# Who spreads the inverse row sums, and where: VectorE into a buffer of its own, with two steps of the opening moved forward

## The chip, the cores and the metric

The kernel runs on one core of a Trainium2 chip. The metric is the device time of one execution in microseconds (us). A core has five engines that run their own instruction streams and wait for each other by semaphores: TensorE (PE, matrix products; PEld is its loading of weights), VectorE (DVE), ScalarE (ACT), GpSimd (POOL) and SyncE (SP, which issues most transfers).

## The reference, cut to what matters

Three stages follow each other: attention with a local window, a dense layer with the mish activation, and a mixture of eight experts of which each token takes one.

```python
scores = scale * q @ k.T + bias          # 2 batches, 8 heads, 768 tokens, 64 per head
scores = where(keep, scores, -1e9)       # 96 local and 8 global keys
a = exp(scores - max(scores))
a = a / (sum(a) + 1e-9)
x = (a @ v)                              # 1536 tokens x 512
h = x @ w_in                             # 512 -> 2048
g = h * tanh(log1p(exp(h)))
x = g @ w_out                            # 2048 -> 512
e = argmax(x @ w_gate); p = softmax(x @ w_gate)[e]
out = p * (max(x @ w1[e], 0) @ w2[e])    # 8 experts, 512 -> 1024 -> 512
```

The change touches the division of `a` by its sum. The kernel multiplies `a @ v` by the inverse of the sum instead.

## The kernel before, in words

**Attention.** The 1536 tokens are 12 tiles of 128. A step `s` is half a tile: four of its eight heads. A step goes through scores on TensorE (`a_S`, L289), row maxima on VectorE (`a_max`, L302), exponentials and row sums on ScalarE (`a_exp`, L313), eight transposes on TensorE (`a_T`, L338 and L340), their copies to SBUF as `PT` on ScalarE (`a_Tev`, L353), and the products with `v` on TensorE (`a_V`, L375), which leave `av`, transposed: channels on the partitions, tokens along the row.

**The inverse row sums.** After the second step of tile `t`, `a_recip(t)` (L318, L319) turns the eight sums per token into their inverses on VectorE, and GpSimd spreads each of them over the 64 channels of its head (L321), into a tile `rs`. The sums have tokens on the partitions and `av` has channels there, so `a_R(t)` transposes the spread tile on TensorE (L327) and ScalarE copies the result back over `rs` (L328). Then `a_x(t)` multiplies `av` by `rs` in place (L388, VectorE), casts the product to the high part `xh` (L389, ScalarE) and subtracts to get the low part `xl` (L390, VectorE). `rs` has one buffer: the spread of a tile waits until L390 of the tile before is through.

**Scaling q.** `prep_qk(t)` scales the q of a tile (L264), on VectorE for tile 0 and on GpSimd for the others. From the fourth tile on it is placed behind the last spread on GpSimd (`gorder`).

**The mixture layer, first part.** Units `u` of one weight block by 256 tokens (two tiles): 24 products `hp` (L421) from `xh`, `xl` and a weight pair `wpair`, the mish chain on ScalarE and VectorE (L448 to L480), and 12 products `acc` (L440) two units later. The weights are 64-bit numbers that are cut to fp32 and split on VectorE (L167, L169, L171, L207) and ScalarE (L205), a chunk at a time; these are called conversion below. Units 0 to 9 run interleaved with the attention of tiles 2 to 11, two steps per unit. From unit 12 on, `x_reload` brings `xh` and `xl` back from DRAM on GpSimd's queue (L403).

**What sets the order.** In the opening (steps 0 to 4, up to `a_x(1)`) the order on TensorE, ScalarE, VectorE and GpSimd is that of the code. It holds warm-up products (`fill`, L843) that compute nothing. Behind the opening a scheduler orders each engine by priorities and its own estimates. Every engine runs its stream in order, and each wait holds up all that stands behind it.

**The prefill.** 24 transfers from one tile of zeros, `z` (L592 to L598), on SP's queue clear the experts' lists in DRAM. `z` comes from the pool `xe` under the tag `x2`, which has three buffers in turn and later holds rows on their way to the experts.

Of the kernel before, what the change touches and what calls it, by code (L numbers as in the profile page):

```python
# [8 lines left out]
F32 = mybir.dt.float32  # L9
# [9 lines left out]
B, H, S, D = 2, 8, 768, 64  # L19
NT, DM, DFF = B * S, H * D, 2048  # L20
# [15 lines left out]
ROW = DM + 2  # L36
# [5 lines left out]
def moe_kernel(ctx, tc, q, k, v, n_global, n_local, w_in, w_out, w_gate, w1, w2, out, dbg=None):  # L42
    nc = tc.nc
# [8 lines left out]
    xe = main.enter_context(tc.tile_pool(name="xe", bufs=3))  # L52
# [6 lines left out]
    ident = const.tile([128, 128], F32, name="ident")  # L59
# [36 lines left out]
    gorder = [None]  # L96
# [117 lines left out]
    at = actx.enter_context(tc.tile_pool(name="at", bufs=2, side="right"))  # L214
# [65 lines left out]
    rbs = {}  # L280
# [28 lines left out]
    def a_exp(s, q_):  # L309
        t, pr = divmod(s, 2)  # L310
        w = geom(t)[1]
        h = 4 * pr + q_
        nc.scalar.activation(out=Ps[s][:, q_, 0:w], in_=Ps[s][:, q_, 0:w], func=AF.Exp,  # L313
                             bias=mxs[s][:, q_:q_ + 1], scale=-1.0, accum_out=rcs[t][:, h:h + 1])

    def a_recip(t):
        su = rcs.pop(t)
        nc.vector.tensor_scalar_add(su, su, 1e-9)  # L318
        nc.vector.reciprocal(su, su)  # L319
        rbs[t] = at.tile([128, 4, 128], F32, tag="rs", name="rs", bufs=1)  # L320
        gorder[0] = nc.gpsimd.tensor_copy(rbs[t].rearrange("p a (b c) -> p (a b) c", c=64),  # L321
                                          su.unsqueeze(2).to_broadcast([128, H, 64])).ins

    def a_R(t):
        rb = ps.tile([128, 4, 128], F32, tag="b", name="rb")
        for p_ in range(4):
            nc.tensor.transpose(rb[:, p_, :], rbs[t][:, p_, :], ident)  # L327
        nc.scalar.copy(rbs[t], rb)  # L328

    pts = {}  # L330
# [504 lines left out]
    with tc.manual_schedule(engines={mybir.EngineType.PE, mybir.EngineType.Activation, mybir.EngineType.DVE, mybir.EngineType.Pool}), tc.tile_pool(name="tmp0", bufs=1, side="right") as tmp0:  # L835
# [34 lines left out]
        for s in range(NS):  # L870
            for q_ in range(2):
                a_exp(s, q_)
            if s:
                fill(4)
                a_T(s - 1, 0)
                a_T(s - 1, 1)
# [4 lines left out]
            if s == 0:  # L881
                for _ in range(6):
                    next(b1, None)
            if s == 4:
                a_x(0)
            if s + 1 < NS:
                a_max(s + 1, 0)
# [17 lines left out]
            if s:  # L905
                fill(3)
                a_V(s - 1)
            if s in (2, 4):
                a_R(s // 2 - 1)
            if s in (2, 3):  # L910
                next_conv(2)
            if s in (1, 2):
# [15 lines left out]
    s = NS  # L928
# [116 lines left out]
    for u in range(u0, NU + 2):  # L1045
        pl, bl, jl = units[u - 2]
        rt = bl - 1 if pl == 2 and bl > 0 else None
        if u < NU:
            p, b, j = units[u]
# [143 lines left out]
    with tc.If(slow > 0):  # L1193
        dense = nc.values_load(flag[0:1, 1:2], min_val=0, max_val=1)
        with tc.If(dense > 0):
            xd = dr.tile([NT, DM], F32, name="xd")
            sld = dr.tile([1, H], F32, name="sld")
            with tc.tile_pool(name="fa", bufs=1) as fa, tc.tile_pool(name="fap", bufs=1, space=PSUM) as fap:
# [13 lines left out]
                for b in range(B):  # L1212
                    with tc.For_i(0, H, 1) as hi_:
# [10 lines left out]
                        for i in range(TPB):  # L1224
# [27 lines left out]
                            su = fa.tile([128, 1], F32, name="fsu")  # L1252
# [15 lines left out]
            with tc.tile_pool(name="fm", bufs=1) as fm, tc.tile_pool(name="fmp", bufs=1, space=PSUM) as fmp:  # L1268
# [16 lines left out]
                with tc.For_i(0, NTILE, 1) as ti_:  # L1285
# [24 lines left out]
                    x2 = fm.tile([128, ROW], F32, name="fx2")  # L1310
# [94 lines left out]
```

## Time and profile before

| | |
|---|---|
| time, three runs | 615.55, 611.99, 615.64 us (median 615.55) |
| profiled execution | 612.52 us, of it 610.8 us span from the first to the last instruction |
| TensorE busy | 588.1 us (96%) |
| VectorE busy | 477.2 us (78%) |
| ScalarE busy | 379.3 us (62%) |
| GpSimd busy | 96.5 us (16%) |
| granted TensorE clock | 0.995 of full speed on average |

Durations below come from the profiled execution. Times are counted from the first instruction. A busy share says little about a stage by itself: matrix products are pipelined, so TensorE can be called busy while it is slowed, and an engine that is idle may have nothing to do. What counts is which engine is waited for in a stretch, and what stands behind the waiting instruction.

### The profile page before, as it was taken

What the parts mean: (1) busy time and instruction counts of PE and PEld (TensorE: products, weight loads), DVE (VectorE), ACT (ScalarE), POOL (GpSimd) and SP (SyncE); (2) the same over time, 40 slices, a digit from 0 to 9 for tenths busy, and PEclk for the clock granted to TensorE, in tenths of its full rate; (3) what the DMA queues carried; (4) which work ended last, traced back from release to release, by engine and by line L of the source; (5) the groups of instructions that cost most, each with busy time, mean ns of one, the idle gap of its engine ahead of it and who ended that gap; (6) DMA issues with size and microseconds to landing.
All of it is one profiled execution on the core that took longest, in us unless ns stands there. A gap on an engine that the chain in (4) does not pass through costs nothing.

```text
span 610.8 us, 12116 instructions
## 1 busy us (share of the span) xinstructions
PE 588.1 (96%) x4374; PEld 528.5 (87%) x4374; DVE 477.2 (78%) x1143; ACT 379.3 (62%) x882; POOL 96.5 (16%) x167
## 2 busy tenths in 40 slices
PE   7989999999999999999999999988999999999994
PEld 6868777777799899999899898878999999999994
DVE  5999999985589999877667677755896678887942
ACT  3768787878767655655555555455664466676731
POOL 3131111120100100000201111121201212113111
PEclk8999999999999999999999999999999999999998
DMA  7975677699768665431332210287676384586300
GB/s 216 313 225 184 225 237 238 204 269 295 208 217 281 195 204 173 139 137 35 105 97 77 88 53 36 56 294 243 210 253 222 134 304 150 207 302 213 123 18 21
DMA packets 54904, 109.93 MB, mean 180 GB/s; under 512 B 5708, under 2 KB 12876, under 8 KB 54835
## 3 DMA queue, kind: packets, MB, share of 16 engines
q1 hardware_dynamic: 49138, 90.18, 44.7%
q0 software_dynamic: 5696, 18.89, 9.3%
q8 instruction: 36, 0.59, 0.4%
q14 instruction: 34, 0.27, 0.1%
HBM read 84.64 MB, written 25.10 MB: 180 GB/s over the span
## 4 chain that ended last, share of the span: by engine, by line
PE 68%; DVE 12%; ACT 7%; DMA 6%; issue 3%; SPq 1%; POOL 1%; DVEq 0%; POOLq 0%; ACTq 0%
PE hp L421 21%; PE acc L440 18%; PE bhp L704 4%; PE bacc L704 4%; DMA bst<-in_moe_w_dram 3%; DVE bw L157 3%; PE av L375 2%; ACT P L313 2%; PE bhp L705 2%; PE bacc L705 2%; DMA xg<-x,dsi 2%; PE warm L843 1%; PE sp L289 1%; PE bhp L707 1%; PE bacc L707 1%
## 5 line engine op out<-in xcount | busy, mean ns | idle before, releaser
L421 PE MATMUL hp<-xh,wpair 128*128 128x256 f32 x768 | 151.6, 287 | 1.9 <-ACT xh L389 1.9
L421 PEld LDWEIGHTS hp<-xh,wpair 128*128 128x128 f32 x768 | 122.1, 188 | 7.6 <-ACT xh L389 3.3
L440 PE MATMUL acc<-wpair,gh 128*128 128x512 f32 x384 | 123.8, 400 | 1.4 <-ACT gh L477 1.4
L421 PE MATMUL hp<-xl,wpair 128*128 128x256 f32 x384 | 108.7, 283 | 0.9 <-DVE xl L390 0.8
L440 PEld LDWEIGHTS acc<-wpair,gh 128*128 128x128 f32 x384 | 68.1, 188 | 16.3 <-issue 2.5
L157 DVE TENSOR_TENSOR bw<-bst,bw 128x512 fp32r<-128x512 f32 x112 | 72.9, 685 | 11.4 <-ACT bw L156 10.8
L448 ACT ACTIVATE e<-hp 128x512 f32<-128x512 f32 x48 | 28.7, 599 | 80.7 <-PE hp L421 80.7
L156 ACT CAST bw<-bst 128x512 fp32r<-128x512 f32 x112 | 64.6, 621 | 21.0 <-PE bhp L708 9.4
L440 PE MATMUL acc<-wpair,gl 128*128 128x512 f32 x192 | 75.4, 393 | 0.0
L421 PEld LDWEIGHTS hp<-xl,wpair 128*128 128x128 f32 x384 | 72.3, 188 | 3.1 <-DVE xl L390 1.9
L704 PE MATMUL bhp<-xc,bw 128*128 128x352 f32 (+4 forms) x192 | 59.3, 364 | 0.7 <-DVE t L739 0.6
L704 PE MATMUL bacc<-hc,bw 128*128 128x352 f32 (+4 forms) x192 | 59.2, 363 | 0.0
L313 ACT ACTIVATE P<-P,mx 128x232 f32<-128x232 f32 (+1 forms) x96 | 44.8, 469 | 16.6 <-DVE mx L302 16.6
L705 PE MATMUL bhp<-xc,bw 128*128 128x176 f32 (+4 forms) x192 | 48.4, 252 | 0.0
L705 PE MATMUL bacc<-hc,bw 128*128 128x176 f32 (+4 forms) x192 | 48.4, 252 | 0.0
L458 DVE SCALAR_TENSOR_TENSOR n<-n,r 128x512 f32<-128x512 f32 x48 | 33.0, 688 | 16.1 <-ACT r L456 15.9
L440 PEld LDWEIGHTS acc<-wpair,gl 128*128 128x128 f32 x192 | 36.1, 188 | 7.5
L480 DVE SCALAR_TENSOR_TENSOR gl<-n,gh 128x512 fp32r<-128x512 f32 x48 | 33.1, 690 | 11.4 <-ACT gh L477 10.2
L452 ACT ACTIVATE n<-e 128x512 f32<-128x512 f32 x48 | 30.3, 632 | 12.0 <-DVE e L450 11.7
L704 PEld LDWEIGHTS bhp<-xc,bw 128*128 128x128 f32 x192 | 36.1, 188 | 1.7 <-DVE t L739 0.8
L705 PEld LDWEIGHTS bacc<-hc,bw 128*128 128x128 f32 x192 | 36.7, 191 | 0.0
L705 PEld LDWEIGHTS bhp<-xc,bw 128*128 128x128 f32 x192 | 36.7, 191 | 0.0
(192 smaller groups left out, 1270.2 us busy)
## 6 DMA issues: line engine op xcount, KB each, us to landing
bst<-in_moe_w_dram SPq DMA_DIRECT2D x56, 512.0 KB
wst<-in_moe_w_in_dram SPq DMA_DIRECT2D x16, 512.0 KB
wst<-in_moe_w_out_dram SPq DMA_DIRECT2D x16, 512.0 KB
xl<-xs POOLq DMA_DIRECT2D x12, 512.0 KB, 4.2
xh<-xs POOLq DMA_DIRECT2D x12, 512.0 KB, 4.9
xpl<-xps SPq DMA_DIRECT2D x24, 256.0 KB
xg<-z SPq DMA_DIRECT2D x24, 224.9 KB
w0f<-in_moe_w_dram SPq DMA_DIRECT2D x8, 512.0 KB
```

The lines of the kernel that those rows point to most:

```text
L156: nc.scalar.copy(hi, src)
L157: nc.vector.tensor_sub(lo, src, hi.bitcast(F32))
L313: nc.scalar.activation(out=Ps[s][:, q_, 0:w], in_=Ps[s][:, q_, 0:w], func=AF.Exp, bias=mxs[s][:, q_:q_ + 1], scale=-1.0, accum_out=rcs[t][ ...
L375: nc.tensor.matmul(av[64 * j:64 * j + 64, 2 * pr + i, :], lhsT=lh, rhs=rh, start=(c == 0), stop=(c == 1))
L421: yield lambda f=f, kk=kk, wi=wi, xx=xx, cs=cs: nc.tensor.matmul(hp[:, f, :], lhsT=w[:, wi, kk, cs], rhs=xx[:, kk, :], start=(kk == 0 and ...
L440: yield lambda f=f, o=o, cs=cs, gi=gi, wi=wi, first=first, last=last: nc.tensor.matmul(accs[b][o], lhsT=gi[:, cs], rhs=w[:, wi, f, :], sta ...
L448: nc.scalar.activation(out=e, in_=hp, func=AF.Exp, scale=-1.0)
L452: nc.scalar.activation(out=n, in_=e, func=AF.Square)
L458: nc.vector.scalar_tensor_tensor(out=n, in0=n, scalar=0.25, in1=r, op0=ALU.add, op1=ALU.mult)
L480: nc.vector.scalar_tensor_tensor(out=gl, in0=n, scalar=-(2.0 ** -80), in1=gh.bitcast(F32), op0=ALU.mult, op1=ALU.subtract)
L704: nc.tensor.matmul(o[:, 0:2 * cap], lhsT=wh, rhs=xc, start=first, stop=False)
L705: nc.tensor.matmul(o[:, 0:cap], lhsT=wl, rhs=xh, start=False, stop=last)
```

## The change

Three things. First, the spread is a VectorE copy into a tile `sp_` from the pool `xe` (tag `x2`), so the source of the transposes is no longer the buffer that `x` is built in; `rs` is now only the target of ScalarE's copy. With the spread gone from GpSimd, `gorder` stays at the last bias copy, and the scaling of q no longer stands behind spreads. Second, in the opening `a_R(0)` and `a_R(1)` stand at the start of steps 2 and 4 instead of behind the products with `v` there. Third, `a_x(0)` stands in step 3 instead of step 4.

```diff
@@ a_recip, a_R
         nc.vector.reciprocal(su, su)
-        rbs[t] = at.tile([128, 4, 128], F32, tag="rs", name="rs", bufs=1)
-        gorder[0] = nc.gpsimd.tensor_copy(rbs[t].rearrange("p a (b c) -> p (a b) c", c=64),
-                                          su.unsqueeze(2).to_broadcast([128, H, 64])).ins
+        sp_ = xe.tile([128, ROW], F32, tag="x2", name="sp_")[:, 0:DM]
+        nc.vector.tensor_copy(sp_.rearrange("p (a b) -> p a b", b=64), su.unsqueeze(2).to_broadcast([128, H, 64]))
+        rbs[t] = sp_
 
     def a_R(t):
         rb = ps.tile([128, 4, 128], F32, tag="b", name="rb")
+        sp_ = rbs[t]
         for p_ in range(4):
-            nc.tensor.transpose(rb[:, p_, :], rbs[t][:, p_, :], ident)
+            nc.tensor.transpose(rb[:, p_, :], sp_[:, p_ * 128:p_ * 128 + 128], ident)
+        rbs[t] = at.tile([128, 4, 128], F32, tag="rs", name="rs", bufs=1)
         nc.scalar.copy(rbs[t], rb)
@@ the opening, for s in range(NS)
             for q_ in range(2):
                 a_exp(s, q_)
+            if s in (2, 4):
+                a_R(s // 2 - 1)
             if s:
                 fill(4)
                 a_T(s - 1, 0)
...
-            if s == 4:
+            if s == 3:
                 a_x(0)
...
                 a_V(s - 1)
-            if s in (2, 4):
-                a_R(s // 2 - 1)
```

Line numbers of the changed kernel are higher by one or two from L321 on: its copy is L321, its transposes are L328, and what was L388 to L390 is L390 to L392. Three places show what that does to the streams.

**Place 1, x of tile 0.** VectorE behind the maxima of step 3, before and then after. L167, L169, L171 and L207 are conversion, L388 (L390 after) is x, L390 (L392 after) is `xl`, and L302 begins the maxima of step 4.

```order
L207 TENSOR_TENSOR wpair_0_302<-cv,wpair_0_302 128x512
L167 TENSOR_SCALAR cv<-wst 128x512 x2
L169 SCALAR_TENSOR_TENSOR cv<-wst,cv 128x512 x2
L171 SCALAR_TENSOR_TENSOR cv<-wst,cv 128x512 x2
L302 ISA P,mx<-sp,ndist 128x232
```

```order
L207 TENSOR_TENSOR wpair_0_302<-cv,wpair_0_302 128x512
L167 TENSOR_SCALAR cv<-wst 128x512 x2
L169 SCALAR_TENSOR_TENSOR cv<-wst,cv 128x512 x2
L171 SCALAR_TENSOR_TENSOR cv<-wst,cv 128x512
L390 TENSOR_TENSOR rs<-av,rs 128x512
L171 SCALAR_TENSOR_TENSOR cv<-wst,cv 128x512
L392 TENSOR_TENSOR xl<-rs,xh 128x4x128
L302 ISA P,mx<-sp,ndist 128x232
```

The product and the difference of tile 0 now stand ahead of the maxima of step 4. ScalarE at the same place, before and then after; L353 (L355 after) copies `PT` of step 2, L389 (L391 after) is `xh`, L205 conversion.

```order
L313 ACTIVATE P,su<-P,mx 128x232 x2
L328 COPY rs<-rb 128x512
L313 ACTIVATE P,su<-P,mx 128x232 x2
L353 COPY PT<-pt 104x512
L353 COPY PT<-pt 128x512
L205 CAST wpair_0_302<-cv 128x512
```

```order
L205 CAST wpair_0_302<-cv 128x512
L313 ACTIVATE P,su<-P,mx 128x232 x4
L391 CAST xh<-rs 128x4x128
L355 COPY PT<-pt 104x512
L355 COPY PT<-pt 128x512
L205 CAST wpair_0_302<-cv 128x512
```

The cast of tile 0 moved to a place directly ahead of the two copies of `PT`; the copy of `rb`, L328, moved forward out of this piece.

**Place 2, x of tile 1.** VectorE from the sums of tile 1 to its product (L388 before, L390 after), before and then after.

```order
L318 TENSOR_SCALAR su<-su 128x8
L319 RECIPROCAL su<-su 128x8
L207 TENSOR_TENSOR wpair_0_302<-cv,wpair_0_302 128x512
L388 TENSOR_TENSOR rs<-av,rs 128x512
L207 TENSOR_TENSOR wpair_0_506<-cv,wpair_0_506 128x512
L167 TENSOR_SCALAR cv<-wst 128x512
L390 TENSOR_TENSOR xl<-rs,xh 128x4x128
L169 SCALAR_TENSOR_TENSOR cv<-wst,cv 128x512
L167 TENSOR_SCALAR cv<-wst 128x512
L171 SCALAR_TENSOR_TENSOR cv<-wst,cv 128x512
L169 SCALAR_TENSOR_TENSOR cv<-wst,cv 128x512
L388 TENSOR_TENSOR rs<-av,rs 128x512
```

```order
L318 TENSOR_SCALAR su<-su 128x8
L319 RECIPROCAL su<-su 128x8
L321 COPY sp__413<-su 128x512
L207 TENSOR_TENSOR wpair_0_302<-cv,wpair_0_302 128x512
L167 TENSOR_SCALAR cv<-wst 128x512
L207 TENSOR_TENSOR wpair_0_508<-cv,wpair_0_508 128x512
L169 SCALAR_TENSOR_TENSOR cv<-wst,cv 128x512
L167 TENSOR_SCALAR cv<-wst 128x512
L171 SCALAR_TENSOR_TENSOR cv<-wst,cv 128x512
L169 SCALAR_TENSOR_TENSOR cv<-wst,cv 128x512
L171 SCALAR_TENSOR_TENSOR cv<-wst,cv 128x512
L390 TENSOR_TENSOR rs<-av,rs 128x512
```

The copy came in, the product and the difference of tile 0 are gone from here, and one more L171 stands ahead of the product of tile 1.

**Place 3, the transposes of tile 1.** TensorE from the products with `v` of step 2 to the scores of step 5 (L289), before and then after. L843 (L845 after) are warm-ups, L338 and L340 (L340 and L342 after) the transposes of P of step 3, L327 (L328 after) those of the spread sums.

```order
L375 MATMUL av<-PT,vv 64x128 x8
L843 MATMUL warm<-ident 128x128 x4
L338 MATMUL pt<-ident,P 104x128 x4
L340 MATMUL pt<-ident,P 128x128 x4
L843 MATMUL warm<-ident 128x128 x3
L375 MATMUL av<-PT,vv 64x128 x8
L327 MATMUL rb<-ident,rs 128x128 x4
L289 MATMUL sp<-kT,qr 128x232 x4
```

```order
L377 MATMUL av<-PT,vv 64x128 x8
L328 MATMUL rb<-ident,sp__413 128x128 x4
L845 MATMUL warm<-ident 128x128 x4
L340 MATMUL pt<-ident,P 104x128 x4
L342 MATMUL pt<-ident,P 128x128 x4
L845 MATMUL warm<-ident 128x128 x3
L377 MATMUL av<-PT,vv 64x128 x8
L289 MATMUL sp<-kT,qr 128x232 x4
```

The transposes moved ahead of one whole step of P and of its products with `v`; those of tile 0 moved in the same way one tile earlier.

On GpSimd the 12 spreads are gone, the scalings of q now follow each other in pairs of tiles, and the memset of `z`, which stood at the start of the stream, stands behind the last of them.

## Rows read from the trace of the kernel before

**Rows 1.** The page, busy time of each engine, its share of the span, and instructions
```profile
PE 588.1 (96%) x4374; PEld 528.5 (87%) x4374; DVE 477.2 (78%) x1143; ACT 379.3 (62%) x882; POOL 96.5 (16%) x167
```

**Rows 2.** Windows: stretch, its length, busy us of each engine, clock, DMA
```profile
core 0: us, PE busy (x) PEld busy (x) DVE busy (x) ACT busy (x) POOL busy (x), PEclk, DMA share, GB/s
40.00:120.00 80.00, 77.33 (x637) 61.67 (x635) 78.15 (x212) 66.74 (x179) 12.12 (x15) 1.00 0.65 214
120.00:160.00 40.00, 38.95 (x312) 30.78 (x308) 27.95 (x85) 30.30 (x84) 4.99 (x5) 1.00 0.98 285
```

**Rows 3.** Timeline around the first spread: start, duration, engine, line, operation, tiles
```profile
16.83 0.38 DVE L167 TENSOR_SCALAR cv<-wst 128x512 int32<-128x512 int32 x1
17.24 0.98 DVE L169 SCALAR_TENSOR_TENSOR cv<-wst,cv 128x512 int32<-128x512 int32 x1
17.64 1.48 POOL L264 TENSOR_TENSOR qr<-qr,qsc 128x512 f32<-128x512 f32 x1
18.25 1.41 DVE L171 SCALAR_TENSOR_TENSOR cv<-wst,cv 128x512 int32<-128x512 int32 x1
```

**Rows 4.** Timeline of the opening, TensorE; in brackets idle time before and its releaser
```profile
15.80 1.54 PE L375 MATMUL av<-PT,vv 8*64 8x128 f32 x16
...
26.75 1.10 PE L375 MATMUL av<-PT,vv 104*64 104x128 f32 x16
...
30.41 1.10 PE L375 MATMUL av<-PT,vv 104*64 104x128 f32 x16
31.60 0.66 PE L327 MATMUL rb<-ident,rs 128*128 128x128 f32 x4
...
33.17 1.16 PE L945 MATMUL wm<-ident 128*128 128x128 f32 x8
35.18 0.39 PE L421 MATMUL hp<-xh,wpair 128*128 128x256 f32 x1 [0.85 <-ACT xh L389]
...
35.91 0.39 PE L421 MATMUL hp<-xl,wpair 128*128 128x256 f32 x1
```

**Rows 5.** Timeline of the opening, the other engines
```profile
24.08 1.28 DVE L171 SCALAR_TENSOR_TENSOR cv<-wst,cv 128x512 int32<-128x512 int32 x2
...
24.74 1.06 ACT L353 COPY PT<-pt 104x512 f32<-104x512 f32 x2
...
27.38 0.17 DVE L318 TENSOR_SCALAR su<-su 128x8 f32<-128x8 f32 x1
...
30.63 0.91 POOL L321 COPY rs<-su 128x512 f32<-128x512 f32 x1 [11.52 <-PE warm L843]
...
33.80 0.68 DVE L388 TENSOR_TENSOR rs<-av,rs 128x512 f32<-128x512 f32 x1
```

**Rows 6.** L450: its group (ns shortest/median/longest), then timeline rows beside GpSimd's
```profile
L450 DVE TENSOR_SCALAR e<-e x48: 412/427/1296, 42.2 to 391.9; 128x512 f32<-128x512 f32 x48
...
67.59 1.04 POOL L264 TENSOR_TENSOR qr<-qr,qsc 128x512 f32<-128x512 f32 x1
67.67 1.24 DVE L450 TENSOR_SCALAR e<-e 128x512 f32<-128x512 f32 x1 [0.52 <-ACT e L448]
...
108.84 0.83 DVE L450 TENSOR_SCALAR e<-e 128x512 f32<-128x512 f32 x1
...
135.25 0.96 DVE L450 TENSOR_SCALAR e<-e 128x512 f32<-128x512 f32 x1 [0.79 <-ACT e L448]
```

**Rows 7.** Groups of one line: ns shortest/median/longest, first and last start, form
```profile
L321 POOL COPY rs<-su x12: 613/874/1124, 17.0 to 161.1; 128x512 f32<-128x512 f32 x12
...
L264 DVE TENSOR_TENSOR qr<-qr,qsc x1: 684/684/684, 8.5 to 8.5; 128x512 f32<-128x512 f32 x1
```

**Rows 8.** Prefill and first re-load: timeline rows, and the page's us to landing (last)
```profile
127.94 10.29 SPq L598 DMA_DIRECT2D xg<-z  x14
...
162.21 0.92 POOL L403 DMA_DIRECT2D xl<-xs  x1
...
179.12 0.28 PE L421 MATMUL hp<-xh,wpair 128*128 128x256 f32 x1
...
xh<-xs POOLq DMA_DIRECT2D x12, 512.0 KB, 4.9
```

## The prediction

> **What bounds the kernel now.** I read the page first, then the windows by stage, then the timeline of the opening. On the page TensorE is busy for 96% of the span [rows 1], so a change can only pay where TensorE waits or fills time. The windows say where that may be [rows 2]. From 40 to 120 us VectorE is busy for 78.15 of 80 us and TensorE for 77.33: both are all but full, and VectorE has 1.85 us to spare in the whole stretch. From 120 to 160 us VectorE has 12 us to spare (27.95 of 40 busy) and TensorE 1.05. Soon after, attention ends and TensorE carries the rest, so what TensorE has lost by then stays in the time. The reader should keep two questions: when does the first mixture product start in the opening, and does VectorE get more work before 120 us?
>
> In the opening TensorE goes from one attention step to the next with warm-up products between them [rows 4]. The first product of the mixture layer starts at 35.18 us, after a wait of 0.85 for xh of token tile 1; the first that needs xl of that tile follows at 35.91. What is late there is x of tile 1 (VectorE, 33.80 [rows 5]), behind its transposes (31.60 [rows 4]), behind GpSimd's spread (30.63 [rows 5]). The sums of tile 1 were taken up at 27.38 [rows 5]. GpSimd was idle, but its spread of tile 1 goes into the one buffer that still holds x of tile 0, and waits until that x has been split.
>
> **The change, part by part.**
>
> *Price of one spread.* On GpSimd it took 0.61 to 1.12 us, 12 times [rows 7]. The trace has no VectorE copy of a spread operand. From below, one-source VectorE instructions of 512 elements took 0.38 and 0.41 [rows 3, 6]; from above, the one that multiplies by a spread operand took 0.68 [rows 7]. A copy has one source, so I take 0.41 and keep 0.68 for the range. Twelve copies are 4.9 us of VectorE work, about nine of them before 120 us. The Trainium skill ("VectorE: DVE Perf Modes", the perf-mode tier table) gives an fp32 copy within SBUF two elements a cycle; by it the price would be the lower one, and 0.38 for a one-source shift agrees [rows 3].
>
> *What VectorE gets back.* A VectorE instruction that starts while GpSimd works is longer by what GpSimd has left: L450 takes 0.41 at its shortest, and 1.24 where it starts 0.08 us after L264 [rows 6]. I went through all VectorE instructions of 512 elements from 17 to 170 us. Five were stretched by the spread itself (first L169 at 17.24, 0.98 instead of 0.68; last L450 at 108.84, 0.83 instead of 0.41 [rows 3, 6]): 1.6 us together. These go. Six were stretched by the scaling of q, L264, that GpSimd does right after the spread (first L171 at 18.25, 1.41 instead of 0.68; last L450 at 135.25, 0.96 [rows 3, 6]): 4.7 us together. The scaling stays on GpSimd, no longer behind a spread, and runs as soon as its q has landed, two tiles in a row; it will meet other VectorE instructions, and I count its 4.7 us as unchanged. The Trainium skill ("SBUF — State Buffer", who interferes with whom) has it that whoever comes second waits for the whole instruction, which these rows agree with, and that VectorE instructions with one SBUF input outside the two-port modes are spared. That is the mechanism of the first rival.
>
> *The opening, in the order of the changed rows.* The transposes of tile 0 (about 0.5 us) stand behind the values of step 0, which end at 17.3 [rows 4]. The copy follows the reciprocal at about 16.9 and ends at 17.3 to 17.6, so TensorE waits 0 to 0.3 us. Scores and maxima of step 3 come 0.5 later, and so does VectorE's conversion work behind them.
>
> Now x of tile 0 stands between two L171 (a pair from 24.08 on before [rows 5]). It starts at 24.08 + 0.6 + 0.5 = 25.2 and ends at 25.8. On ScalarE the cast to xh now stands ahead of the two copies of PT that started at 24.74 [rows 5], and waits for x: cast 25.8 to 26.4, PT 26.4 to 27.5. TensorE needs both for the values of step 2, which began at 26.75 [rows 4]: they begin at 27.5. Behind PT on ScalarE stand a conversion cast (0.6) and the last two exponentials of tile 1 (1.0), until 29.1; the sums were taken up at 27.38 before. Sum, reciprocal and copy on VectorE are done at 29.9. TensorE has finished its values at 28.6 and waits 1.3 us for that copy, with the warm-ups, P and the values of step 3 queued behind the transposes. From values to values it needed 26.75 to 30.41, 3.7 us [rows 4]: the values of step 3 come at 27.5 + 3.7 + 1.3 + 0.5 = 33.0. From there to the end of the warm-ups it was 30.41 to 34.3 with 0.6 for the transposes that are gone from this place [rows 4]: 33.0 + 3.3 = 36.3. So the first mixture product starts at about 36.3 instead of 35.18.
>
> Is x of tile 1 there by then? After the copy VectorE has eight conversion instructions first (six at 0.6, two at 0.35: 4.4 us): 29.9 + 4.4 = 34.3, x to 35.0, xh to 35.6, then one conversion, one maximum, xl to 36.6. So xh is in time for 36.3, and xl comes at 36.6; before it was 35.18 and 35.91. The opening loses **0.7 to 1.1 us; I take 1.0**. The wait at 35 us goes, but two of its size take its place earlier: for PT at 27 and for the copy of tile 1 at 29. In exchange VectorE has done one more conversion by then.
>
> *From 40 to 120 us.* Seven copies at 0.41 are 2.9; two of the five relieved instructions lie here, 0.6. VectorE's work grows by 2.3 us, and it has 1.85 to spare [rows 2]. TensorE loses 0.4 if all of that can be used, 2.3 if none: I take 0.5, near the lower end, because TensorE is nearly full itself and because conversions, which are needed only later, stand further back in the changed order. After 120 us nothing: the last three copies lie in 12 us of spare time [rows 2]; without it they would cost 1.2.
>
> *What else moves.* The prefill's zero tile shares a pool of three buffers with the new tile, so its memset now stands behind the last scaling on GpSimd, and the 24 writes from it on SP's queue (14 of them from 127.94 on [rows 8]) come 20 to 30 us later, among the first re-loads of x. The first re-load has 17 us from its issue (162.21) to its use (179.12) and lands in about 5 [rows 8], so I cost it at nothing; without that cover TensorE would stop at 179 us.
>
> **Sum.** 1.0 and 0.5 are 1.5 us more. The profiled execution took 612.5, so it would be 614.0. The three runs lie between 612.0 and 615.6 with a mean of 614.4, and the profiled one stands 3 below their median of 615.55. I set the sum on the mean: **615.9 us**.
>
> **The rivals.**
> - *Faster, the spared meetings.* The scaling now mostly meets the maxima of L302 or idle time, and its 4.7 us go with the spreads' 1.6. VectorE gains 6.3 and pays 4.9, 1.4 net; an L450 such as that of 67.67, between product and mish, gets shorter by 0.83 twice, and an opening that breaks even saves the 1.5 of the sum: 614.4 - 1.4 - 1.7 = 611.3. For it: L302 reads PSUM and is never stretched in the trace. Against: nearly all else on VectorE reads two SBUF tiles, and the scalings come in pairs. Chance 0.18.
> - *Slower, the queues of ScalarE and VectorE.* The copy costs 0.68 and VectorE's growth goes through one for one: 7 x 0.68 - 0.6 = 4.2; the opening loses the whole 1.7 us by which PT is late. That is 5.9: 620.3. It decides from a copy of 0.6 us on. Chance 0.12.
> - *The prefill's writes delay the re-loads.* Sixteen of the writes fall between 169 and 182 us; a re-load would have to take over three times its 5 us. Then perhaps 3 us more than the forecast's mean, 617.4. Chance 0.08.
> - The forecast has the rest, 0.62.
>
> **Chances.** The range reaches from the first rival to the second: 610.4 to 620.6, about 0.9 below and 0.3 above their centres. A measurement of this kernel can tell about 1% (6.2 us) from no change. Faster by that needs 609.4, beyond the first rival: 0.04. Slower needs 621.7, the upper part of the second: 0.10. The rest is 0.86.
>
> **What would show it.** Right: the copy at 0.38 to 0.45 us; TensorE waiting for ScalarE's PT at about 27 and for the copy at about 29 us; the first mixture product at 36 to 37; L264 on GpSimd in pairs. Wrong: a copy of 0.6 or more; a first product before 35; few long instructions on VectorE and less than 80 us for the work from 40 to 120; TensorE waiting at 179 us.

## The result and the profile after

The changed kernel took 617.86 us (median of 22 runs, 613.78 to 622.01), the kernel before 613.22 us on the same chip (22 runs, 611.55 to 616.01). The ratio is 1.0068, with a 95% interval of 1.0048 to 1.0087: 0.7% slower, 4.2 us between the means of the runs. The forecast was 615.9 us and no change beyond 1%.

The profiled execution of the changed kernel took 619.03 us, of it 617.2 us span. The page of it, busy time of each engine:

```profile
PE 589.6 (96%) x4374; PEld 530.9 (86%) x4374; DVE 480.7 (78%) x1155; ACT 380.2 (62%) x882; POOL 85.4 (14%) x155
```

Against [rows 1] twelve instructions have gone from GpSimd to VectorE. TensorE is busy 1.5 us longer in a span that is 6.4 us longer, so it has waited more. The first question is where. The first mish exponential of each unit (L448 before, L450 after) serves as a mark along the kernel:

| unit | before, us | after, us | later by |
|---|---|---|---|
| 0 | 40.83 | 44.96 | 4.13 |
| 3 | 81.58 | 87.19 | 5.61 |
| 6 | 121.65 | 126.38 | 4.73 |
| 9 | 161.95 | 166.18 | 4.23 |
| 24 | 249.96 | 254.19 | 4.23 |
| 47 | 391.29 | 395.51 | 4.22 |

In this execution all of it is there at the first mixture unit. The stretch with the interleaved attention moves the loss up and down and ends 0.1 us worse. From unit 9 to unit 47 nothing changes. (The last 2.2 us of the span came at 400 to 412 us, in the hand-over to the experts, where this execution had a lower clock, 0.72 from 406 to 412 us against 1.00 before. That the table's 4.23 us equal the 4.2 us between the means is partly chance: 1.0 of them belongs to this execution's clock in the first 14 us, as shown below.) The windows of after, with the columns of [rows 2]:

```profile
core 0: us, PE busy (x) PEld busy (x) DVE busy (x) ACT busy (x) POOL busy (x), PEclk, DMA share, GB/s
40.00:120.00 80.00, 75.86 (x634) 61.41 (x636) 76.94 (x221) 64.52 (x174) 8.78 (x10) 1.00 0.64 211
120.00:160.00 40.00, 39.19 (x316) 31.18 (x314) 30.06 (x92) 33.18 (x89) 0.78 (x4) 1.00 0.52 179
```

VectorE is not fuller from 40 to 120 us than before (76.94 against 78.15). The opening on TensorE, to be laid beside [rows 4] (start, duration, engine, line, tiles; in brackets the idle time before and its releaser):

```profile
16.83 1.54 PE L377 MATMUL av<-PT,vv 8*64 8x128 f32 x16
...
19.19 0.66 PE L328 MATMUL rb<-ident,sp__286 128*128 128x128 f32 x4 [0.83 <-DVE sp__286 L321]
...
28.87 1.36 PE L377 MATMUL av<-PT,vv 104*64 104x128 f32 x16
31.73 1.04 PE L328 MATMUL rb<-ident,sp__413 128*128 128x128 f32 x4 [1.49 <-DVE sp__413 L321]
32.56 1.91 PE L845 MATMUL warm<-ident 128*128 128x128 f32 x8
34.27 1.06 PE L340 MATMUL pt<-ident,P 128*104 128x128 f32 x4
...
36.40 1.10 PE L377 MATMUL av<-PT,vv 104*64 104x128 f32 x16
...
39.32 0.37 PE L423 MATMUL hp<-xh,wpair 128*128 128x256 f32 x1
...
39.94 0.38 PE L423 MATMUL hp<-xl,wpair 128*128 128x256 f32 x1
```

TensorE now waits twice for VectorE's copies. Behind the second wait stand the transposes of the exponentials of step 3 (34.27) and their product (36.40). The first mixture product starts at 39.32 instead of 35.18. ScalarE and VectorE in the same stretch, beside [rows 3, 5]:

```profile
17.81 1.04 POOL L264 TENSOR_TENSOR qr<-qr,qsc 128x512 f32<-128x512 f32 x1
...
18.16 0.98 DVE L321 COPY sp__286<-su 128x512 f32<-128x512 f32 x1
...
27.71 0.62 ACT L391 CAST xh<-rs 128x512 fp32r<-128x512 f32 x1 [3.02 <-DVE rs L390]
28.24 1.06 ACT L355 COPY PT<-pt 104x512 f32<-104x512 f32 x2
...
30.80 0.17 DVE L318 TENSOR_SCALAR su<-su 128x8 f32<-128x8 f32 x1 [0.47 <-ACT P L313]
31.24 0.43 DVE L321 COPY sp__413<-su 128x512 f32<-128x512 f32 x1
...
31.96 2.39 POOL L264 TENSOR_TENSOR qr<-qr,qsc 128x512 f32<-128x512 f32 x2 [12.33 <-DMA qr<-in_q_dram]
32.30 1.15 DVE L167 TENSOR_SCALAR cv<-wst 128x512 int32<-128x512 int32 x1
33.37 1.52 DVE L207 TENSOR_TENSOR wpair<-cv,wpair 128x512 fp32r<-128x512 f32 x1
...
37.68 0.68 DVE L390 TENSOR_TENSOR rs<-av,rs 128x512 f32<-128x512 f32 x1
```

The reader should see three things. ScalarE stands idle for 3.02 us ahead of xh of tile 0, with PT behind it. The first copy meets a scaling of q and takes 0.98 instead of 0.43. And a pair of scalings lies between the second copy and x of tile 1 and stretches two conversions there by 0.73 and 0.84.

A last view is the copy's and the mish instruction's group (ns shortest/median/longest):

```profile
L321 DVE COPY sp__601<-su x1: 415/415/415, 44.7 to 44.7; 128x512 f32<-128x512 f32 x1
...
L452 DVE TENSOR_SCALAR e<-e x48: 414/427/634, 45.6 to 396.1; 128x512 f32<-128x512 f32 x48
```

Eleven of the twelve copies took 0.41 to 0.43 us, like the one shown. The mish instruction that GpSimd stretched to 1.30 before [rows 6] now takes 0.63 at most.

### The profile page after: what moved, and what is told of

Same layout as the page of the kernel before. It is cut to its first block, busy times and chain, and to the rows that moved or that the text cites. A ratio compares the mean times of both kernels' runs of the same rounds, so it can differ in the third digit from the quotient of the medians.

```text
span 617.2 us, 12103 instructions
## 1 busy us (share of the span) xinstructions
PE 589.6 (96%) x4374; PEld 530.9 (86%) x4374; DVE 480.7 (78%) x1155; ACT 380.2 (62%) x882; POOL 85.4 (14%) x155
## 4 chain that ended last, share of the span: by engine, by line
PE 75%; DVE 10%; ACT 5%; DMA 4%; issue 3%; SPq 1%; POOL 1%; DVEq 0%; POOLq 0%; ACTq 0%
PE hp L423 22%; PE acc L442 19%; PE bhp L706 5%; PE bacc L706 5%; PE av L377 3%; PE bhp L707 2%; PE bacc L707 2%; PE sp L289 2%; DMA bst<-in_moe_w_dram 2%; PE bhp L709 1%; PE bacc L709 1%; PE bacc L711 1%; PE bhp L711 1%; PE bacc L710 1%; PE bhp L710 1%
## 5 line engine op out<-in xcount | busy, mean ns | idle before, releaser
L450 ACT ACTIVATE e<-hp 128x512 f32<-128x512 f32 x48 | 28.7, 599 | 79.9 <-PE hp L423 79.9
L156 ACT CAST bw<-bst 128x512 fp32r<-128x512 f32 x112 | 64.5, 620 | 19.6 <-PE bhp L710 9.6
L442 PEld LDWEIGHTS acc<-wpair,gl 128*128 128x128 f32 x192 | 36.3, 189 | 7.6
L707 PEld LDWEIGHTS bacc<-hc,bw 128*128 128x128 f32 x192 | 36.7, 191 | 0.0
L707 PEld LDWEIGHTS bhp<-xc,bw 128*128 128x128 f32 x192 | 36.7, 191 | 0.0
L706 PEld LDWEIGHTS bacc<-hc,bw 128*128 128x128 f32 x192 | 36.1, 188 | 0.6
```

The costliest lines, as they stand in the source:

```text
L156: nc.scalar.copy(hi, src)
L442: yield lambda f=f, o=o, cs=cs, gi=gi, wi=wi, first=first, last=last: nc.tensor.matmul(accs[b][o], lhsT=gi[:, cs], rhs=w[:, wi, f, :], sta ...
L450: nc.scalar.activation(out=e, in_=hp, func=AF.Exp, scale=-1.0)
L706: nc.tensor.matmul(o[:, 0:2 * cap], lhsT=wh, rhs=xc, start=first, stop=False)
L707: nc.tensor.matmul(o[:, 0:cap], lhsT=wl, rhs=xh, start=False, stop=last)
```

## The experiments

Two numbers are read from each profile. One is the first mixture product. The other is **TensorE's idle time from 16 us to the first mish exponential of unit 9**, because that is the stretch in which the marks above move and TensorE carries what follows. It comes from one window per kernel. Here are those of before and of after: stretch, its length, busy time of TensorE, and the other engines as above.

```profile
16.00:161.95 145.95, 141.17 (x1171) 112.79 (x1168) 129.56 (x368) 114.57 (x313) 25.05 (x32) 1.00 0.77 242
```

```profile
16.00:166.18 150.18, 142.56 (x1179) 114.96 (x1178) 133.66 (x384) 116.25 (x316) 15.06 (x23) 0.99 0.62 204
```

TensorE is idle for 4.78 us before (145.95 less 141.17) and for 7.62 after: 2.84 us more. The other 1.39 of the 4.23 us is busy time. Of it 1.0 was work left over at 16 us: the sums of tile 0 were taken up at 17.52 instead of 16.51, since the granted clock was 0.50 of full speed from 8 to 14 us (its lower level throughout) where before it was 0.72 on average. The remaining 0.4 is slower work from 32 to 36 us: the clock was at 0.50 from 32 to 34 us, after TensorE had been busy for only 0.51 us of the 2 us before. The windows of the changed kernel, TensorE alone (stretch, length, busy time, clock, DMA):

```profile
8.00:14.00 6.00, 4.72 (x28) 0.50 1.09 304
30.00:32.00 2.00, 0.51 (x8) 0.96 0.85 246
32.00:34.00 2.00, 2.00 (x11) 0.50 0.13 53
```

| run | what it is | ratio (95%) | first product, us | TensorE idle, us |
|---|---|---|---|---|
| before | | 1 | 35.18 | 4.78 |
| after | | 1.0068 (1.0048 to 1.0087) | 39.32 | 7.62 |
| e1_zlate | before, zero tile late | 0.9999 (0.9968 to 1.0029) | 34.70 | 5.62 |
| e2_zfill | after, identity as late as before | 1.0066 (1.0034 to 1.0098) | 39.17 | 9.70 |
| e3_spread | copy on VectorE alone | 1.0007 (0.9976 to 1.0038) | 36.22 | 6.27 |
| e4_moves | the moves alone | 1.0052 (1.0030 to 1.0073) | 37.00 | 8.83 |
| e5_xbehind | after, xh behind PT | 1.0062 (1.0031 to 1.0093) | 44.42 | 10.42 |
| e6_rback | after, transposes back | 1.0010 (0.9975 to 1.0046) | 37.18 | 5.31 |
| e7_rbehind | after, transposes behind pt | 0.9991 (0.9969 to 1.0014) | 37.54 | 5.05 |
| e8_hold | after, scaling held | 1.0154 (1.0109 to 1.0198) | 40.12 | 10.48 |
| e9_r0first | transposes of tile 0 early | 1.0031 (1.0005 to 1.0057) | 35.80 | 6.21 |
| e10_r1first | transposes of tile 1 early | 1.0074 (1.0041 to 1.0107) | 38.08 | 8.00 |
| e11_rbx4 | transposes behind pt, x in step 4 | 0.9997 (0.9971 to 1.0023) | 38.81 | 5.34 |
| e12_rbx4w | the same, more warm-ups | 0.9981 (0.9961 to 1.0002) | 36.34 | 5.08 |

Two cautions belong to this table. The last two columns come from one execution each, and the first product carries what that execution lost before 20 us, mostly by its clock: the sums of tile 0 came between 15.59 us (e9_r0first) and 19.15 us (e8_hold). Counted from them, the first product comes after 18.7 us before, 21.8 after, 21.0 in e7_rbehind, 20.4 in e10_r1first and 20.2 in e9_r0first, so it does not sort the ratios. A better mark is the sums of tile 2, counted in the same way: 21.2 us before and at most 23.3 in the runs with ratios up to 1.0031 (24.1 in e7_rbehind is the one exception), 24.7 or more in those with 1.0052 and above. The attention itself is what falls behind.

The second caution is the clock as a rival. The mean granted clock of the changed kernel's 22 runs is 0.988, that of the groups of the kernel before, measured beside the experiments, 0.990 to 0.992. Some of the 0.7% may lie there. It is not what makes the loss: the runs of e4_moves below have 0.991, as before, at a ratio of 1.0052.

### Which part of the change: e1 to e4

The first theory was that the loss is made in the opening by the moved steps and by the zero tile: its memset no longer stands ahead of the identity on GpSimd, so the warm-ups begin at 1.67 instead of 2.13 us and end sooner. The rival was that twelve copies on VectorE are the loss.

**e1_zlate**: the kernel before with the zero tile's memset behind the last spread.

```diff
     z = xe.tile([112, ROW], F32, tag="x2", name="z")
-    nc.gpsimd.memset(z[:, 0:DM], 0.0)
+    with tc.issue_after(gorder[0]):
+        nc.gpsimd.memset(z[:, 0:DM], 0.0)
...
```

> The kernel before with one edit: the prefill's zero tile is cleared behind GpSimd's last spread instead of at the start of its stream. Theory A (the zero tile's memset held the identity matrix back; without it the twelve warm-up products start at 1.67 us instead of 2.13 and end before 6.2, the gap to the first scores is over 3 us, and the clock is at its lower level when they start): first scores take about 2.2 us instead of 1.3, the first mish exponential starts 0.8 to 1.3 us later than 40.83, and the time rises by about 1 us (ratio 1.001 to 1.003). Theory B (the place of the memset is of no account, as the prediction had it): first mish exponential within 0.2 us of 40.83, ratio 1.000.

The ratio is 0.9999: the zero tile's place costs nothing. The warm-ups began at 1.67 here too.

**e2_zfill**: the changed kernel with a memset of the same size in the old place, into a buffer that is overwritten later.

```diff
+    nc.gpsimd.memset(ndist[0:112, 0:DM], 0.0)
     make_identity(nc, ident)
```

> The changed kernel with one memset of the zero tile's size (into a tile that is written over later) at the start of GpSimd's stream. Theory A: warm-up products start about 2.1 and end about 7.3 us again, the first mish exponential comes at 43.6 to 44.2 instead of 44.96, the time falls by about 1 us against the changed kernel (ratio to the kernel before 1.004 to 1.006). Theory B: nothing moves, 44.96 and 1.0068.

The warm-ups began at 2.13 as before, the clock from 8 to 14 us was that of before (0.72), and the sums of tile 0 came at 16.56 against 16.51. Still the ratio is 1.0066. So neither the zero tile nor the clock at the start is the loss. The second wait is there without any fall of the clock, and the first product is no sooner:

```profile
31.70 0.66 PE L328 MATMUL rb<-ident,sp__414 128*128 128x128 f32 x4 [1.49 <-DVE sp__414 L321]
...
39.17 0.39 PE L423 MATMUL hp<-xh,wpair 128*128 128x256 f32 x1 [1.28 <-ACT xh L391]
```

**e3_spread**: the changed kernel with the opening of before, so that only the copy's engine and buffer differ, and with them the places of the scalings and of the zero tile on GpSimd.

```diff
-            if s in (2, 4):
-                a_R(s // 2 - 1)
...
-            if s == 3:
+            if s == 4:
                 a_x(0)
...
                 a_V(s - 1)
+            if s in (2, 4):
+                a_R(s // 2 - 1)
```

> The first part of the change alone: VectorE copies into a buffer of its own, and the opening stands as before (transposes of the spread sums behind the products with v, x of tile 0 in step 4). Theory A (the loss is made in the opening by the two moves and by the zero tile; the copies on VectorE cost next to nothing): first mish exponential at 41 to 42.3 us, no growth from there to the tenth unit, ratio 1.001 to 1.003. Rival C (the twelve copies on a full VectorE are the loss): ratio 1.004 or more, and the lateness against the kernel before grows by 2 us or more between the first and the tenth mish exponential.

The ratio is 1.0007. Twelve copies on VectorE cost nothing that can be measured, although the first took 1.30 beside a scaling: the transposes that read it came at the end of the step, and waited for nothing. The first mish exponential came at 43.39 us, later than the expected 41 to 42.3, and the lateness was made up by unit 9: lateness at unit 0 need not stay in the time.

**e4_moves**: the kernel before with the moves alone (the reverse of the diff above); the spread stays on GpSimd in the one buffer.

> The second part alone: GpSimd spreads into the single buffer as before, but the transposes stand at the start of steps 2 and 4 and x of tile 0 stands in step 3. Theory A: ScalarE's PT of step 2 waits for x of tile 0, TensorE then waits for PT (about 1 to 2 us) and for the spread of tile 1 (1.5 us or more), the first mish exponential comes at 43 to 45 us, ratio 1.003 to 1.007. Rival C: 41 to 41.5 us and ratio 1.000 to 1.001.

The ratio is 1.0052. Most of the loss, if not all within the intervals, lies in the moves. TensorE waits at the same two places, now for GpSimd:

```profile
17.71 0.66 PE L327 MATMUL rb<-ident,rs 128*128 128x128 f32 x4 [0.38 <-POOL rs L321]
...
30.81 0.66 PE L327 MATMUL rb<-ident,rs 128*128 128x128 f32 x4 [2.05 <-POOL rs L321]
```

### Which of the moves: e5 to e8

Two theories were left. X: xh of tile 0 queues on ScalarE ahead of PT (the 3.02 us). R: the transposes of the inverse sums, written ahead of pt (the transposes of the exponentials) and av (the products with v), hold them on TensorE while a copy is awaited.

**e5_xbehind**: the changed kernel, the first x written behind the two copies to PT.

```diff
-            if s == 3:
-                a_x(0)
...
                 a_Tev(s - 1, 1)
+            if s == 3:
+                a_x(0)
```

> The changed kernel, with the first x left in step 3, but written behind the two copies that put the transposed exponentials into PT, so that on ScalarE xh of tile 0 stands behind PT instead of ahead of it. Theory X (the loss is a queue on ScalarE: in the changed kernel xh of tile 0 waits there 3.02 us for x, which stands on VectorE behind the splitting of weights, and PT, the exponentials of step 3 and so the second sums stand behind it): the wait of 3.02 us before PT goes, the sums of tile 1 stand at about 28 us instead of 30.80, the first hp about 3 us sooner than 39.32, ratio to the kernel before 1.000 to 1.002. Theory R (the loss comes from the transposes of the inverse sums that now stand ahead of pt and av on TensorE and hold them while the copy is awaited): the ratio stays at 1.005 to 1.007.

The ratio is 1.0062, but this run does not tell X from R. PT no longer waits for x; the last exponentials of tile 1 do, since x and xh now stand ahead of those. The sums of tile 1 came at 33.06 and met a pair of scalings, which put the copy at 36.07:

```profile
33.06 0.17 DVE L318 TENSOR_SCALAR su<-su 128x8 f32<-128x8 f32 x1
33.14 1.56 DVE L169 SCALAR_TENSOR_TENSOR cv<-wst,cv 128x512 int32<-128x512 int32 x1
34.62 0.19 DVE L319 RECIPROCAL su<-su 128x8 f32<-128x8 f32 x1
34.74 1.41 DVE L171 SCALAR_TENSOR_TENSOR cv<-wst,cv 128x512 int32<-128x512 int32 x1
36.07 0.42 DVE L321 COPY sp__413<-su 128x512 f32<-128x512 f32 x1
```

TensorE waited 5.27 us for that copy, with all that stands behind the transposes. It shows how much hangs on one copy once they stand first.

**e6_rback**: the changed kernel, transposes back at the end of steps 2 and 4, the first x still in step 3.

```diff
-            if s in (2, 4):
-                a_R(s // 2 - 1)
...
                 a_V(s - 1)
+            if s in (2, 4):
+                a_R(s // 2 - 1)
```

> The changed kernel with the transposes of the inverse sums put back to the end of steps 2 and 4, and the first x left in step 3 ahead of PT. Theory X: ScalarE still waits about 3 us for x before PT, the sums of tile 1 stay later than 30 us, ratio 1.004 to 1.006. Theory R: the transposes hold nothing any more, first hp at 36 us or sooner, ratio 1.000 to 1.002.

The ratio is 1.0010, where R expected it; the first product, expected at 36 us or sooner, came at 37.18 in an execution whose sums of tile 0 were 1.2 us late. No transposes wait, and pt and the product of step 3 no longer stand behind the copy (30.11 to 30.54 us):

```profile
30.03 0.60 PE L340 MATMUL pt<-ident,P 128*104 128x128 f32 x4
...
31.66 1.10 PE L377 MATMUL av<-PT,vv 104*64 104x128 f32 x16
32.70 0.65 PE L328 MATMUL rb<-ident,sp__413 128*128 128x128 f32 x4
```

X's wait went too, from 3.02 to 0.62 us, which X had not expected: with the first transposes out of the way the scores of step 3 came sooner, and so did the conversion ahead of x on VectorE. Most of ScalarE's wait was thus a result of the early transposes of tile 0 (2.67 us with them alone in e9_r0first below, 0.62 without in e10_r1first).

**e7_rbehind**: the changed kernel, transposes in the same steps but behind pt and the scores.

```diff
-            if s in (2, 4):
-                a_R(s // 2 - 1)
             if s:
                 fill(4)
                 a_T(s - 1, 0)
                 a_T(s - 1, 1)
             if s and s + 1 < NS:
                 a_S(s + 1)
+            if s in (2, 4):
+                a_R(s // 2 - 1)
```

> The changed kernel with the transposes of the inverse sums still in steps 2 and 4 ahead of the values' products, but behind the transposes of the exponentials and the scores, so that those are not held while the copy is awaited. Theory X: ScalarE's wait of 3 us ahead of PT stays, ratio 1.004 to 1.007. Theory R: the 0.83 and 1.49 us of TensorE's waits shrink and the exponentials' transposes of step 4 stand before the copy, ratio 1.000 to 1.003.

The ratio is 0.9991. TensorE is through with pt when it comes to the copy of tile 1, and waits 0.40 us for it:

```profile
30.27 0.60 PE L340 MATMUL pt<-ident,P 128*104 128x128 f32 x4
...
31.71 0.63 PE L328 MATMUL rb<-ident,sp__413 128*128 128x128 f32 x4 [0.40 <-DVE sp__413 L321]
...
32.94 0.66 PE L289 MATMUL sp<-kT,qr 64*128 64x232 f32 x4
33.56 1.37 PE L377 MATMUL av<-PT,vv 104*64 104x128 f32 x16
```

ScalarE still waits 1.94 us for x ahead of PT, two thirds of the 3.02, so X falls: most of its wait is there and the loss is not. R holds. The run has a second difference, though: half of the scores of step 5 (L289) now stand ahead of the products with v of step 3 (L377), where they stand behind them in the kernel before and in the changed one. In e11_rbx4 and e12_rbx4w below all of them do. What that is worth alone was not measured; e6_rback is free of it.

**e8_hold**: the changed kernel, with the scaling of q held behind VectorE's copies.

```diff
-        nc.vector.tensor_copy(sp_.rearrange("p (a b) -> p a b", b=64), su.unsqueeze(2).to_broadcast([128, H, 64]))
+        gorder[0] = nc.vector.tensor_copy(sp_.rearrange("p (a b) -> p a b", b=64), su.unsqueeze(2).to_broadcast([128, H, 64])).ins
```

> The changed kernel with the scaling of q on GpSimd from the fourth tile on held behind the latest copy on VectorE, as in the kernel before it was held behind GpSimd's spread. Both theories: the first copy no longer runs beside a scaling and takes 0.41 to 0.45 us instead of 0.98, the first transposes of the inverse sums come some 0.5 us sooner, and the ratio falls by 0.001 at most, to 1.005 to 1.007. If the meeting of the first copy with the scaling were the loss, the ratio would be 1.002 or less.

The ratio is 1.0154, and the run says nothing on the meeting that it was made for. The edit also moved the scaling of the third tile ahead of two bias copies on GpSimd, where it waited 5.09 us for its q; the first maxima with a wide window came late and the sums of tile 0 at 19.15. Its first copy took 0.43 alone, its second 1.31 beside a pair of scalings.

### Which transposes, and a better place: e9 to e12

**e9_r0first** and **e10_r1first**: the changed kernel with one of the two transposes early, the other at the end of its step.

```diff
-            if s in (2, 4):
+            if s == 2:
                 a_R(s // 2 - 1)
...
                 a_V(s - 1)
+            if s == 4:
+                a_R(s // 2 - 1)
```

This is e9_r0first; e10_r1first has 4 and 2 the other way round.

> The changed kernel with the early place kept for the transposes of tile 0 alone (head of step 2); those of tile 1 stand at the end of step 4 again, behind the values' products. The runs so far: with both early the ratio to the kernel before is 1.0068, with both at the end of their steps 1.001. If the hold of tile 0 is the loss (TensorE waits 0.83 us there, and the scores of step 3, the weights' splitting and the first x all come after it): first hp at 38.5 us or later, ratio 1.004 to 1.007. If the hold of tile 1 is the loss (1.49 us of TensorE, and pt, PT and the values' product behind it before the second x): first hp at 37.5 us or sooner, ratio 1.000 to 1.003.

> The changed kernel with the early place kept for the transposes of tile 1 alone (head of step 4); those of tile 0 stand at the end of step 2 again. If the hold of tile 0 is the loss: ratio 1.000 to 1.003, first hp at 37.5 us or sooner. If the hold of tile 1 is the loss: TensorE waits 1 to 2 us for the second copy with pt behind it, first hp at 38.5 us or later, ratio 1.004 to 1.007. If each carries half, both this run and the one before lie at 1.003 to 1.004.

Tile 0's early place has 1.0031, tile 1's 1.0074, as much as the whole change. Beside e6_rback, which has neither (1.0010), only tile 1's stands out: the place of its transposes, and what it holds on TensorE, is the loss, and what tile 0's adds is within the intervals. All these runs have x of tile 0 in step 3; none has the early transposes with x in step 4, so whether they cost as much there is open. TensorE in e10_r1first:

```profile
30.70 0.63 PE L328 MATMUL rb<-ident,sp__413 128*128 128x128 f32 x4 [1.58 <-DVE sp__413 L321]
...
32.06 0.60 PE L340 MATMUL pt<-ident,P 128*104 128x128 f32 x4
...
33.69 1.10 PE L377 MATMUL av<-PT,vv 104*64 104x128 f32 x16
...
38.08 0.39 PE L423 MATMUL hp<-xh,wpair 128*128 128x256 f32 x1 [1.21 <-ACT xh L391]
```

From the copy of tile 1 to the first product there is now a chain: copy, transposes, warm-ups, pt, the copy to PT, the product with v, scores, warm-ups. In e6_rback four of these are over before the copy is needed.

**e11_rbx4**: transposes behind pt and the scores, first x in step 4 as before the change. **e12_rbx4w**: the same with 20 in place of 12 of the first warm-ups.

```diff
-            if s in (2, 4):
-                a_R(s // 2 - 1)
...
-            if s == 3:
+            if s == 4:
                 a_x(0)
+            if s in (2, 4):
+                a_R(s // 2 - 1)
```

```diff
-NWARM = 12
+NWARM = 20
```

> The copy on VectorE into its own buffer as in the change; the transposes of the inverse sums stand in steps 2 and 4 behind the transposes of the exponentials and the scores and ahead of the values' products; the first x stands in step 4, as before the change. If only the place on TensorE decides: no transposes wait ahead of work that is ready, ScalarE does not wait for x ahead of PT, the sums of tile 1 stand at about 28 us, ratio 0.997 to 1.000. If VectorE's queue sets the second x (as with the opening of before, where its work ran without a gap up to x at 34.84 us): ratio 0.999 to 1.002.

> The same as the run before with 20 in place of 12 of the first warm-up matmuls, which fill the idle time before the first scores: the clock stays at 1.00 through 8 to 14 us instead of 0.50, and the scores of step 2 come about 0.9 us sooner than behind a low clock. If the early clock reaches the first x: ratio 0.001 to 0.002 below the run before. If what comes after is set by VectorE and by loads: the same ratio as the run before within 0.001.

0.9997 and 0.9981. Neither can be told from the kernel before at 95%, though e12_rbx4w (611.57 us against 613.34, 0.9961 to 1.0002) is the fastest of all. In it the clock stood at 1.00 from 8 to 14 us and the sums of tile 0 came at 15.64. The gain over e11_rbx4 is 0.0016, the size expected if the early clock counts, and the mean granted clock of the runs rose with it, from 0.992 to 0.995; but the intervals overlap. No version that beats both kernels is shown. In e11_rbx4 VectorE's own queue set the second x, at 37.42 after the copy at 29.83; a pair of scalings from 32.13 on, 2.61 us long, lies between.

## Why the prediction was right or wrong

The time lies 2 us above the forecast, within its range and within 1% of no change. The mechanism was named in part, and one term was far too small. Part of the nearness is luck: the sum of 1.5 us was set on the 614.4 us of three runs, where the 22 runs of the kernel before have a mean of 613.5. The change costs 4.2 us, nearly three times the sum.

**The price of a copy: right.** 0.41 was taken, 0.41 to 0.43 measured, eleven times of twelve. The lower end is the right one. The Trainium skill ("VectorE: DVE Perf Modes", the perf-mode tier table) gave that end for an fp32 copy, and the trace agrees with 0.41 to 0.43.

**From 40 to 120 us, 0.5 us more: small, as forecast.** It was 0.1 between unit 0 and unit 9. VectorE got some of the copies' time back: of the stretched mish instructions none is left. TensorE waits for PT and x at other places than before, the longest 1.80 us for xh at 66 us, and loses nothing on balance. With the copies alone (e3_spread) the stretch from unit 0 to unit 9 was even shorter, 119.77 against 121.12 us.

**The scalings of q, 4.7 us counted as unchanged: mis-sized, and put nowhere.** They did come in pairs, as forecast, all of them before 80 us. Summed over the stretched VectorE instructions they cost about 6.2 us. The trace of the kernel before has seven such instructions and 5.2 us, not six and 4.7: an L450 at 83.12 us that took 0.92 beside a scaling was left out. What mattered is where: 0.56 fell on the first copy and 0.73 and 0.84 on conversions between the second copy and x of tile 1, in a queue for which the prediction had taken undisturbed durations. The Trainium skill ("SBUF — State Buffer", who interferes with whom) has VectorE, in its two-port modes, and GpSimd take turns at a shared pair of ports for whole instructions, and the 0.98 of the first copy beside 0.43 of the second agrees.

**The opening, 1.0 us: the term that failed.** The chain was forecast step by step, and most of the steps occurred. One did not: TensorE was to wait for PT at 27 us, but its own scores and warm-ups ahead of the values of step 2 came late as well, and it waited 0.1 us. The table takes the 1.0 us off with which this execution began late.

| step | forecast, us | measured less 1.0, us | late by |
|---|---|---|---|
| x of tile 0 | 25.2 | 26.0 | 0.8 |
| values of step 2 | 27.5 | 27.9 | 0.4 |
| sums of tile 1 taken up | 29.1 | 29.8 | 0.7 |
| copy of tile 1 done | 29.9 | 30.7 | 0.8 |
| x of tile 1 | 34.3 | 36.7 | 2.4 |
| first mixture product | 36.3 | 38.3 | 2.0 |

The lateness arises in two places. Ahead of x of tile 0 it is the first copy: "TensorE waits 0 to 0.3 us" was 0.83, since the copy met a scaling; where it met none, in e9_r0first, the wait was 0.39. Ahead of x of tile 1, the eight conversion instructions, put at 4.4 us (its own terms, six at 0.6 and two at 0.35, give 4.3), took 6.0, of it 1.57 us by the two met conversions. That these two meetings made the first product late is read from rows; no run took them away without moving something else (e8_hold moved too much). Alone they do not make the kernel slower: in e7_rbehind both first copies (0.91 and 1.21 us) met a scaling, x of tile 1 came 19.6 us after the sums of tile 0 against 20.2 after, and the ratio is 0.9991.

**TensorE "waits 1.3 us for that copy, with the warm-ups, P and the values of step 3 queued behind the transposes": right, and the heart of the matter.** 1.49 was measured. The runs show that this order is the loss: with it 1.0074 (e10_r1first), without it 1.0010 and 0.9991 (e6_rback, e7_rbehind). The prediction priced the wait once, on TensorE. It did not price that the same order makes pt, PT and the product of step 3 follow the copy where they had run beside it. The attention behind them is late too: the sums of tile 2 came 25.8 us after those of tile 0, against 21.2 before and 22.6 in e6_rback. That TensorE then lacks work to catch up with is argued from this, not shown.

**The first product is not the measure.** The prediction took its start for the loss of the opening. e7_rbehind and e11_rbx4 start it at 37.54 and 38.81 us, e11_rbx4 hardly sooner than after, and lose nothing in the end. They win 2 us back by unit 9 (118.99 and 119.18 us from unit 0 to unit 9 against 121.22). The 1.80 us at 66 us is one wait that the changed kernel and e10_r1first have, while the longest for xh in e7_rbehind is 0.5 us; why the order in the opening decides on it was not followed further. TensorE's idle time over the stretch sorts the runs: 6.3 us or less with ratios up to 1.0031, 7.6 or more with 1.0052 and above.

**The rivals.** The faster one did not come: the spared meetings were taken by others. The slower one, with the copy at 0.68 and all of PT's lateness, stands at 620.3 us, farther from the 617.86 than the forecast, and its condition, a copy of 0.6 us or more, was met by one copy of twelve, beside a scaling. The late prefill, at 617.4, is nearest in number, by luck, for it cost nothing: its writes stood from 161 us on among the re-loads [rows 8], and the marks stay 4.23 us late from unit 9 on. With the zero tile late alone the ratio is 0.9999 (e1_zlate).

## What to carry to other kernels

An instruction that waits costs what is queued behind it on its own engine. When a step is moved forward so that its result "stands sooner", put it behind the work that is ready already: the same transposes cost 0.7% ahead of such work and nothing behind it. And when an engine loses a task, look at what it does with the freed time; here GpSimd ran its scalings in pairs, straight into VectorE's chain. By themselves these meetings cost nothing that a run shows (e3_spread, e7_rbehind); they made late what other work then waited for.

## What the runs showed of the hardware

- A VectorE copy of 128x512 fp32 from an operand with each value repeated 64 times took 0.41 to 0.43 us; the same spread took GpSimd 0.61 to 1.12 [rows 7].
- It is stretched by GpSimd like other VectorE work: 0.91 to 1.31 us where it met a scaling.
- The granted clock from 8 to 14 us, behind the gap after the first warm-ups, differs from one execution to the next for the same instructions in the same order. It was 0.50 in the changed kernel and 1.00 in e9_r0first, which is the same up to step 4: the lower of the two levels, 1.2 GHz, against 2.4. The sums of tile 0 came at 17.52 and 15.59 us. Two profiles of such an opening can differ by 2 us where the programs do not differ.

```profile
1.67 4.30 PE L845 MATMUL warm<-ident 128*128 128x128 f32 x24 [1.67 <-POOL ident masks.py:199]
9.28 2.19 PE L289 MATMUL sp<-kT,qr 64*128 64x136 f32 x16 [3.31 <-DVE qr L264]
```

```profile
1.67 5.49 PE L845 MATMUL warm<-ident 128*128 128x128 f32 x24 [1.67 <-POOL ident masks.py:199]
9.28 1.20 PE L289 MATMUL sp<-kT,qr 64*128 64x136 f32 x16 [2.12 <-issue]
```

These are the warm-ups and the first scores on TensorE, above in the changed kernel and below in e9_r0first: the scores start at 9.28 us in both, and take 2.19 us at the low clock and 1.20 at the high one. TensorE had stood idle for 3.31 us ahead of them in the changed kernel and for 2.12 us in e9_r0first.
